# Weight pieces get tiles of their own, order and engines are written down step by step, and constant products fill TensorE's early gaps

## The chip, the cores and the metric

One core of one Trainium2 chip runs the kernel. The metric is the device time of one execution in microseconds; for the kernel before it is the median of three runs. A profile is taken of one execution.

## What is computed

Three parts follow each other, all in float32: attention with a mask of blocks of 64, a channel mix, and a token and channel mixer.

```python
def _attn_ref(q, k, v) -> np.ndarray:
    B, H, S, D = q.shape
    block = 64
    scale = 1.0 / np.sqrt(D)
    scores = scale * np.matmul(q, k.transpose(0, 1, 3, 2))
...
    mask = block_i >= block_j
    scores = np.where(mask, scores, -1000000000.0)
    scores = scores - np.max(scores, axis=-1, keepdims=True)
    attn = np.exp(scores)
    attn = attn / (np.sum(attn, axis=-1, keepdims=True) + 1e-09)
    return np.matmul(attn, v).astype(np.float32)
...
def _moe_ref(x, mu_k, mu_r, w_k, w_v, w_r) -> np.ndarray:
    B, S, D = x.shape
    x_prev = np.concatenate([np.zeros((B, 1, D), dtype=np.float32), x[:, :-1, :]], axis=1)
    xk = mu_k * x + (1.0 - mu_k) * x_prev
    xr = mu_r * x + (1.0 - mu_r) * x_prev
    k = np.maximum(xk @ w_k, 0.0)
    v = k * k @ w_v
    r = 1.0 / (1.0 + np.exp(-(xr @ w_r)))
    return (r * v).astype(np.float32)
...
def _moe2_ref(x, w_tok1, w_tok2, w_ch1, w_ch2) -> np.ndarray:
    xt = x.transpose(0, 2, 1)
    h = np.maximum(xt @ w_tok1, 0.0) @ w_tok2
    u = x + h.transpose(0, 2, 1)
    h2 = np.maximum(u @ w_ch1, 0.0) @ w_ch2
    return (u + h2).astype(np.float32)
```

The sizes are B = 4, H = 8, S = 576, D = 64; the model width is 512, the channel mix is 1024 wide, the mixer 256 over tokens and 1536 over channels.

## The kernel before

**Arithmetic.** A float32 product is made from parts: an operand is split into a high part that TensorE takes at its fast rate and a low part, the rest. Each group then takes three products: high by high (`mm_high`, L1024), low by high (`mm_low`, L1029) and high by low. `L1037` is the same for the others. VectorE, ScalarE and POOL make the parts: `xh` is a cast (L1005), `xl` a subtraction (L1009).

**Attention.** A batch is taken in two halves of the tokens, and each of them in four pairs of heads (`a000` to `a313`: batch, half, pair). A unit of a pair goes: scores on TensorE into `s` (L729), mask (L758), largest (L764), its negative as bias `nb` (L771, L773), exponentials on ScalarE into `p` (L783), sums (L791, L796), reciprocal (L802), the scaled high and rest in half precision into `pin` (L808, L814), a transposing DMA into `pt`, and the products with `vb` (L911). For the first half of batch 0 the probabilities are instead turned on TensorE by a diagonal `dg` of the reciprocal sums (L835 on POOL or L837 on VectorE, rotation L844, eviction `tf` L849, products L901). `vb` is v scaled by a power of two that is found from its largest value: a diagonal `vd` on POOL (L623), a gather on TensorE (L629), short scalings on VectorE. The sums go into `xt`, and `mix` makes `xk` and `xr` out of it (L993, L999, L1005, L1009).

**Mixing and mixer.** Channel mix (`channel_mix`), then for each batch the token part of the mixer (`front`), and for five stretches of tokens the channel part (`back`). These are most of TensorE's work.

**Weights.** `load_split` stages a matrix piece by piece: `split_chunk` loads a piece as three bytes a value (L552), casts its top part (L559), joins it with the rest on VectorE (L562), casts the high part (L568) and subtracts for the low part (L571). The first two matrices (`w_r`, `w_k`) have pieces of 410 columns and use memory that later holds `kh` and `kl`, four places in two tiles (`place`, `homes`); `w_v` uses `qkl`.

**What sets the order.** No engine's code is written in its final order. Each operation is a `step` with an engine, a cost and a key, and `Plan.schedule` gives each engine, step by step, what is ready and has the lowest key, with a model of costs, buffers, queues and TensorE's two speeds. `Plan.run` then writes the instructions in order of the planned starts. The keys come from due times that are worked out from tables in `PLAN` (`shift`, `fine`, `lead_begin` and others), and whether VectorE or another engine takes an operation from shares.

Of the kernel before, what the change touches and what calls it, by code (L numbers as in the profile page):

```python
# [39 lines left out]
SHARED = {"top", "join", "high", "low", "first", "second", "two", "diag", "here", "k_high", "k_low", "rest", "bias", "sums", "power"}  # L40

PLAN = dict(
    wr=-88.407, cpr=3.57, qt=2.2538, a0=87.407, lead=60.32, sh=0.57, xr=13.29, xk=-2.9382, cs=410, cv=256, wk=-50.94,
    wv=-0.88, cpk=1.6637, cpv=2.1596, p1_act=(0, 1, 2, 3, 4), p1_first=(0, 1, 2, 3, 4), xl_d=(0, 2), kl_d=(1, 3, 5),
    kh_a=(1, 2, 4, 6, 7), xh_d=(1, 3), mp=(), qk_a=(0, 1), ql_d=(0, 1), sh_r=(0.0733, 0, 0), sh_k=(0, 0, 0.58),
    sh_v=(0.02, 0, 0), sh_m=(0.35, 0, 0.41), first=38.34, sq_v=(), sq_a=(1, 2, 5, 6), p_ps=(1,), p_pf=(), nb_a=(1, 4),
    sm_a=(1,), ot_a=(1,), nq=(0, 1), dg_a=(), dg_g=(1,), ev_a=(0, 1), sq_1=(), fifo=("xh", "xl", "l", "o", "xt0",
    "xt1", "qkh", "uh"), ft=3.02, fd=27.39, cw=3.3876, tfr=23.04, lx=0.15, lpe=0.2, lse=0.12, land=2.31,

    fine={  # L50
        "a000": {"attention.edge": 28.99, "load_qk.whole": 3.33, "load_v_early.early": 1.77, "pv.products": -27.39,
        "pv.total": -40.77, "unit.bias": 16.3, "unit.diag": -28.96, "unit.evict": 42.0, "unit.exps": -9.13,
        "unit.inverse": -14.81, "unit.largest": 43.59, "unit.mask": 21.28, "unit.rotate": -0.91, "unit.scores": 16.31,
        "unit.sums": 46.99},
        "a001": {"attention.edge": -15.34, "load_qk.whole": 11.15, "load_v_early.early": 20.2, "pv.products": -0.07,
        "pv.total": 5.35, "unit.bias": 12.43, "unit.diag": 10.15, "unit.exps": -0.52, "unit.inverse": -12.18,
        "unit.largest": -6.57, "unit.mask": -0.59, "unit.rotate": 0.51, "unit.scores": 61.26, "unit.sums": -42.15},
        "a002": {"attention.edge": -2.39, "load_qk.whole": 1.24, "load_v_early.early": -81.65, "pv.products": -1.83,
        "pv.total": 2.38, "unit.bias": -19.03, "unit.diag": 6.6, "unit.evict": 7.45, "unit.exps": -1.93,
        "unit.inverse": 0.62, "unit.largest": -54.46, "unit.mask": 85.09, "unit.rotate": -12.99, "unit.scores": 23.8,  # L60
        "unit.sums": 87.92},
        "a003": {"attention.edge": -20.22, "load_qk.whole": -9.52, "load_v_early.early": -59.81, "pv.products": 36.55,
        "pv.total": 14.52, "unit.bias": 4.07, "unit.diag": 1.45, "unit.exps": -6.02, "unit.inverse": -86.56,
        "unit.largest": 2.37, "unit.mask": 7.52, "unit.rotate": -47.64, "unit.scores": -6.87, "unit.sums": 186.98},
        "a010": {"attention.edge": 5.12, "load_qk.whole": 9.68, "load_v.gather": 33.57, "load_v.largest": -4.86,
        "load_v.load": -4.39, "load_v.one": -28.07, "load_v.power": -78.48, "load_v.scale": -1.59, "load_v.spread":
        37.85, "load_v.two": 31.18, "pv.products": -2.0, "pv.total": 68.43, "unit.bias": -0.69, "unit.exps": -18.8,
        "unit.first": 176.41, "unit.inverse": 2.98, "unit.largest": 7.85, "unit.mask": 2.4, "unit.scores": 1.17,
        "unit.second": 0.37, "unit.sums": -4.36, "unit.turn": 49.55},
        "a011": {"attention.edge": 5.78, "load_qk.whole": -0.1, "load_v.gather": -0.4, "load_v.load": -13.43,  # L70
        "load_v.one": 0.85, "load_v.power": 31.47, "load_v.scale": -24.07, "load_v.spread": 10.15, "load_v.two":
        -40.58, "pv.products": 8.74, "pv.total": -0.55, "unit.bias": 16.5, "unit.exps": 22.85, "unit.first": 23.58,
        "unit.inverse": -15.47, "unit.largest": -9.04, "unit.mask": -10.34, "unit.scores": 0.48, "unit.second": -3.54,
        "unit.sums": 26.67, "unit.turn": 50.3},
        "a012": {"attention.edge": 3.0, "load_qk.whole": -23.78, "load_v.gather": -36.47, "load_v.largest": -0.16,
        "load_v.load": -9.38, "load_v.one": 9.22, "load_v.power": 13.36, "load_v.scale": 37.23, "load_v.spread":
        24.22, "pv.products": -4.89, "pv.total": -6.71, "unit.bias": 6.93, "unit.exps": 39.76, "unit.first": 9.47,
        "unit.inverse": 18.71, "unit.largest": -15.32, "unit.mask": 6.23, "unit.scores": -0.44, "unit.second": 123.91,
        "unit.sums": 51.69, "unit.turn": -18.01},
        "a013": {"attention.edge": 17.9, "load_qk.whole": 4.76, "load_v.gather": 1.97, "load_v.largest": 0.17,  # L80
# [1562 lines left out]
```

## Time and profile before

| | us |
|---|---|
| median of three runs | 804.49 (804.41 to 807.11) |
| the profiled execution: span from the first to the last instruction | 802.7 |
| what lies around the span (median less span) | 1.8 |
| TensorE busy in the span | 768.6 |
| VectorE busy | 470.9 |
| ScalarE busy | 416.0 |
| POOL busy | 155.1 |

The profile is of one execution, so terms that are read from it make up its span, and the 1.8 us is added to come to a run's time. TensorE is PE in the rows, VectorE DVE, ScalarE ACT. Busy times are the union of an engine's instructions, a wait is idle time with the instruction that ended it, and in a timeline like instructions that follow each other stand as one row. A tile's number is left out of its name.

### The profile page before, as it was taken

How to read it: one execution, taken by the hardware profiler on the slowest of the kernel's cores; microseconds unless marked ns; L12 is line 12 of the kernel's file. 1: busy time of each engine (PE TensorE's matmuls, PEld its weight loads, DVE VectorE, ACT ScalarE, POOL GpSimd, SP SyncE). 2: the span in 40 equal slices, each digit the busy share in tenths (PEclk: the TensorE clock that was granted, in tenths of full speed). 3: DMA queues.
4: the chain of work that ended last, by engine and by line, in shares of the span. 5: the costliest groups of instructions: out<-in, count | busy, mean ns of one | idle time of the engine just before them, and what ended most of it. 6: DMA issues, size and time to landing. Idle time of an engine off the chain costs nothing.

```text
span 802.7 us, 16092 instructions
## 1 busy us (share of the span) xinstructions
PE 768.6 (96%) x6120; PEld 665.8 (83%) x6120; DVE 470.9 (59%) x1189; ACT 416.0 (52%) x1074; POOL 155.1 (19%) x202
## 2 busy tenths in 40 slices
PE   5469999999999999999999999999999999999998
PEld 3246898889998999999989889998888888888886
DVE  7898898899998789882654588612211302301210
ACT  6887978788879787883555565502101201300100
POOL 5532322212124032322424122200000000000000
PEclk9987999999999999999999999999999999999999
DMA  8849946676858777453542745200000010000001
GB/s 287 293 132 162 190 116 141 122 169 121 170 126 124 142 138 172 75 88 80 202 147 88 267 125 150 75 27 1 14 27 1 17 36 14 1 26 14 1 26 40
DMA packets 130670, 83.25 MB, mean 104 GB/s; under 512 B 104352, under 2 KB 112160, under 8 KB 130080
## 3 DMA queue, kind: packets, MB, share of 16 engines
q1 hardware_dynamic: 130592, 82.22, 42.1%
q8 instruction: 48, 0.79, 0.4%
q14 instruction: 30, 0.25, 0.1%
HBM read 48.11 MB, written 9.44 MB: 72 GB/s over the span
## 4 chain that ended last, share of the span: by engine, by line
PE 85%; ACT 6%; DMA 4%; DVE 4%; issue 1%; POOL 0%; SPq 0%; DVEq 0%; ACTq 0%; POOLq 0%
PE b L1037 37%; PE l L1024 20%; PE l L1029 10%; PE s L729 5%; PE o L911 5%; PE b L1232 3%; PE b L1211 3%; ACT p L783 1%; DMA wst<-in_w_k 1%; DMA x<-xd 1%; PE b L1187 1%; DVE pin L814 1%; DVE nm L764 1%; DMA qkf<-in_kq 1%; DMA pt<-pin 1%
## 5 line engine op out<-in xcount | busy, mean ns | idle before, releaser
L1303 ACT ACTIVATE wy<-b 128x512 fp32r<-128x512 f32 (+1 forms) x60 | 33.3, 555 | 212.1 <-PE b L1037 210.8
L1037 PE MATMUL b<-uh,wx 128*128 128x512 f32 (+1 forms) x480 | 139.3, 372 | 0.0
L1024 PE MATMUL l<-xh,wx 128*128 128x256 f32 (+1 forms) x768 | 124.7, 302 | 0.8 <-DVE ve L635 0.4
L1024 PEld LDWEIGHTS l<-xh,wx 128*128 128x128 f32 x768 | 108.2, 189 | 6.8 <-issue 2.1
L1037 PE MATMUL b<-wy,c2a 128*128 128x512 f32 (+1 forms) x460 | 110.6, 367 | 0.0
L1037 PEld LDWEIGHTS b<-uh,wx 128*128 128x128 f32 x480 | 87.3, 188 | 17.3 <-issue 0.2
L1037 PEld LDWEIGHTS b<-wy,c2a 128*128 128x128 f32 x460 | 79.2, 189 | 15.3
L1318 DVE TENSOR_TENSOR x<-b,x 128x256 f32<-128x256 f32 (+7 forms) x32 | 13.5, 454 | 118.7 <-PE b L1037 118.7
L1024 PE MATMUL l<-kh,wy 128*128 128x256 f32 (+1 forms) x512 | 76.6, 299 | 0.1
L1037 PE MATMUL b<-gx,wx 128*128 128x512 f32 x192 | 75.4, 393 | 0.0
L783 ACT ACTIVATE p<-s,nb 128x128 f32<-128x128 f32 (+4 forms) x120 | 67.5, 566 | 11.6 <-DVE nb L773 6.0
L814 DVE SCALAR_TENSOR_TENSOR pin<-p,rs,pin 128x384 f16<-128x384 f32 (+3 forms) x104 | 66.6, 660 | 9.6 <-ACT pin L808 8.9
L1024 PEld LDWEIGHTS l<-kh,wy 128*128 128x128 f32 x512 | 69.9, 189 | 2.3 <-issue 0.9
L1029 PE MATMUL l<-xl,wx 128*128 128x320 f32 (+1 forms) x384 | 67.8, 298 | 0.0
L808 ACT ACTIVATE pin<-p,rs 128x384 f16<-128x384 f32 (+3 forms) x104 | 62.1, 622 | 9.1 <-DMA pt<-pin 5.8
L764 DVE TENSOR_REDUCE nm<-s 128x2 f32<-128x256 f32 (+4 forms) x80 | 63.8, 800 | 3.5 <-PE s L729 2.8
L1029 PEld LDWEIGHTS l<-xl,wx 128*128 128x128 f32 x384 | 56.1, 188 | 3.0 <-issue 2.4
L1306 DVE SCALAR_TENSOR_TENSOR wy<-b,wy 128x512 fp32r<-128x512 f32 (+1 forms) x28 | 16.1, 576 | 69.0 <-ACT wy L1303 68.9
L911 PEld LDWEIGHTS <-vb 128*64 128x64 f16 x1824 | 46.8, 113 | 9.9 <-issue 6.8
L911 PE MATMUL o<-pt,vb 128*64 128x128 f16 (+1 forms) x1824 | 53.3, 215 | 0.7 <-DMA pt<-pin 0.7
L1121 POOL TENSOR_TENSOR kl<-kt,kh 128x256 fp32r<-128x256 f32 (+1 forms) x40 | 35.1, 881 | 65.7 <-ACT kh L1118 40.5
L1009 POOL TENSOR_TENSOR xl<-mt,xh 128x256 fp32r<-128x256 f32 (+1 forms) x32 | 30.2, 944 | 87.5 <-DVE xh L1005 40.7
(123 smaller groups left out, 1385.5 us busy)
## 6 DMA issues: line engine op xcount, KB each, us to landing
wst<-in_w_c SPq DMA_DIRECT2D x24, 256.0 KB, 2.8
qkf<-in_kq SPq DMA_DIRECT2D x12, 480.0 KB, 4.4
v<-in_v SPq DMA_DIRECT2D x16, 320.0 KB, 3.1
x<-xd SPq DMA_DIRECT2D x4, 1152.0 KB, 8.1
wst<-in_w_c2a SPq DMA_DIRECT2D x18, 256.0 KB, 3.1
qkl<-in_w_v SPq DMA_DIRECT2D x16, 256.0 KB, 3.8
wst<-in_w_k SPq DMA_DIRECT2D x9, 410.0 KB, 4.1
qkf<-in_kq SPq DMA_DIRECT2D x12, 256.0 KB, 2.9
```

The source lines that it names most:

```text
L729: self.nc.tensor.matmul(o, q[e, q0:q0 + P], k[e, k0:k1], start=n == 0, stop=n == len(terms) - 1)
L764: nc.vector.tensor_reduce(out=c["nm"][:, :nh], in_=m, axis=AX.XY if j == 4 else AX.X, op=ALU.max, negate=True)
L783: nc.scalar.activation(out=c[x], in_=s, func=AF.Exp, scale=0.125, bias=c["nb"][:, x:x + 1], accum_out=c["sm"][:, x:x + 1],)
L808: nc.scalar.activation(out=like(pin[:, :n]), in_=c[x], func=AF.Copy, scale=rs)
L814: nc.vector.scalar_tensor_tensor(out=like(pin[:, w:w + n]), in0=c[x], scalar=rs, in1=like(pin[:, :n]), op0=ALU.mult, op1=ALU.subtract)
L911: nc.tensor.matmul(o[hh * D:hh * D + D, q0:q0 + rows], v[:, i, y, hh, :], st["pt", hh, j][:, x * (j + 1) + i, :], start=i == x == y == 0, ...
L1009: (nc.vector if i in pl["xl_d"] else nc.gpsimd).tensor_tensor(out=l, in0=x[i], in1=raw(x["h"][i]), op=ALU.subtract)
L1024: self.nc.tensor.matmul(ps, ww[:, k, :], x[0][k], start=k == 0 and n == 0, stop=False)
L1029: self.nc.tensor.matmul(ps, w[0][:, k, :], x[1][k], start=False, stop=k == kt - 1)
L1037: self.nc.tensor.matmul(ps, ww[k], xx[k], start=k == 0 and n == 0, stop=k == kt - 1 and n == 2)
L1121: (nc.vector if m in pl["kl_d"] else nc.gpsimd).tensor_tensor(out=part("kl")[:, m, :], in0=c["q", m], in1=raw(c["kh"][:, m, :]), op=ALU.su ...
L1303: nc.scalar.activation(out=gh(m), in_=d["g", m][:, :n], func=AF.Relu)
```

## The change

Its parts, in the order of the diff below:

- The tables of `PLAN` and the keys go. Each step has a number, and two lists have an entry for each number: `RANK` is its key, and `ON` the engine letter of the steps that may run on more than one (`"any"`). The helpers `copy`, `less` and `scale` write the operation for the engine that is named.
- The model of TensorE's two speeds goes out of `schedule`.
- `Plan.run` takes a function `fill`. Where TensorE's plan has a gap before a step, until 90 us of the plan, it calls `fill` once for each 0.085 us of the gap beyond 0.15. A fill is a product of ones (128 x 128) by ones (128 x 192, bf16) into columns 320 to 511 of an accumulator `o` that no step reads or writes.
- The pieces of `w_r` and `w_k` get three tiles of their own (`stage0` to `stage2`) in place of four places in the memory of `kh` and `kl`.
- The accumulators `o` are two named tiles; the DMA scratch is 1024.

```diff
+FILL = (4.0, 90.0)
...
+RANK = [int(x) for x in """
+15 0 23 3 5 12 17 21 6 7 1 9 2 35 24 28 29 33 36 37 39 44 46 50 49 54 59 26 31 34 40 57 42 61 75 79 82 80 85 94
...
+ON = "".join("""
+-----------------V--A-A-A-A---V--A-A-A-A---A-----A--A-A-A-A---A--A-A-A-V---A-----A--V-V-A-A---A--A-A-V-A---A----
...
-    def step(self, eng, cost, key, fn, *args, r=(), w=(), after=(), hold=(), dma=0.0, alone=False, mode=""):
+    def step(self, eng, cost, fn, *args, r=(), w=(), after=(), hold=(), dma=0.0, alone=False, mode=""):
...
-            key -= PLAN["lead_begin"].get(kind, 0.0)
-        key -= PLAN["fine"].get(self.group, {}).get(kind, 0.0)
-        s = Step(len(self.steps), eng, cost, key - PLAN["shift"].get(self.group, 0.0), fn, args, dma)
-        s.kind, s.group = kind, self.group
-        s.shared, s.mode = shared, mode
+        alts = None
+        if eng == "any":
+            alts = cost
+            eng = ON[n] if ON else next(iter(alts))
+            cost = alts[eng]
+        share = lambda e: e == "G" or e == "V" and name[-1] in SHARED and not alone
+        s = Step(n, eng, cost, RANK[n] if RANK else n, fn, args, dma)
+        s.kind, s.group = f"{name[1]}.{name[-1]}" if len(name) > 2 else "", self.group
+        s.alts, s.shares = alts, share
+        s.shared, s.mode = share(eng), mode
...
-    def run(self):
-        order = self.schedule()
-        for s in order:
-            s.fn(*s.args)
+    def run(self, fill):
+        last, until = FILL
+        for s in self.schedule():
+            if s.eng == "PE":
+                for _ in range(int((min(s.start, until) - last - 0.15) / 0.085)):
+                    fill()
+                last = s.end
+            s.fn(*s.args, *(s.eng if s.alts else ()))
 
...
+    def copy(self, e, out, x):
+        (self.nc.scalar.copy if e == "A" else self.nc.vector.tensor_copy)(out, x)
+
+    def less(self, e, out, a, b):
+        (self.nc.vector if e == "V" else self.nc.gpsimd).tensor_tensor(out=out, in0=a, in1=b, op=ALU.subtract)
+
...
-        def low():
-            (nc.vector if low_v else nc.gpsimd).tensor_tensor(
-                out=part(1), in0=s["mid"].bitcast(F32), in1=raw(part(0)), op=ALU.subtract
-            )
+        def low(e):
+            self.less(e, part(1), s["mid"].bitcast(F32), raw(part(0)))
...
-        step(*(("V", c_v(k)) if low_v else ("G", c_g(k))), key, low, r=[z] + t[0], w=t[1])
+        step("any", both(v=c_v(k), g=c_g(k)), low, r=[z] + t[0], w=t[1])
 
...
-        self.ones = pool.tile([P, P], BF16, name="ones", bufs=1)
+        self.ones = pool.tile([P, 512 - NT], BF16, name="ones", bufs=1)
+        self.o = [self.ps_o.tile([P, 512], F32, name=f"o{x}", bufs=1) for x in range(BUFS["o"])]
...
+    def fill(self):
+        self.nc.tensor.matmul(self.o[0][:, NT:], self.ones[:, :P], self.ones, start=True, stop=True)
...
-        homes = [Buf(tag) for tag in ("kh", "kl")]
-        tiles = {}
-        half = NF * NT // 2
-        turns = itertools.cycle(range(4))
-
-        def place(x):
-            a = x // 2
-            if a not in tiles:
-                tiles[a] = self.mp.tile([P, NF * NT], U32, tag=("kh", "kl")[a], name="wst", bufs=1)
-            return tiles[a][:, x % 2 * half:(x % 2 + 1) * half]
-
-        def spare(x):
-            return place(x)[:, half - pl["cs"]:]
-
-        for x in range(4):
-            step("G", 0.3, -1e3, lambda x=x: nc.gpsimd.memset(spare(x), 0), w=[(homes[x // 2], ("t", x % 2))])
+        cs = CS
+        turns = itertools.cycle(range(NSTAGE))
+        self.stage = [self.ap.tile([P, 3 * cs + 2], U32, name=f"stage{x}") for x in range(NSTAGE)]
+        for x, z in enumerate(self.stage):
+            step("G", 0.3, nc.gpsimd.memset, z[:, 2 * cs + 2:], 0, w=[(f"stage{x}", "t")])
 
         def early():
             x = next(turns)
-            return lambda: place(x), (homes[x // 2], x % 2), lambda: spare(x), (homes[x // 2], ("t", x % 2))
+            z = self.stage[x]
+            return lambda: z, (f"stage{x}", "z"), lambda: z[:, 2 * cs + 2:], (f"stage{x}", "t")
 
         def staged(pool, tag, size):
...
-        self.plan.run()
+        self.plan.run(self.fill)
...
+NSTAGE = 3
...
-    nc = bacc.Bacc("TRN2", target_bir_lowering=False, num_devices=1)
+    nc = bacc.Bacc("TRN2", target_bir_lowering=False, num_devices=1, dynamic_dma_scratch_size=1024)
```

The instructions move as follows; each place is shown before and after.

The first is TensorE's queue where the first mixing product stands (`L1024` before, `L928` after; both `mm_high`); these are six rows of before from the last products of the first half's attention on. `pt` is a transposed probability tile.

```order
L911 MATMUL o<-pt_637,vb 64x128
L729 MATMUL s<-qk 128x512 x2
L729 MATMUL s<-qk 128x288 x2
L1024 MATMUL l<-xh,wx 128x256 x4
L911 LDWEIGHTS vb
L911 MATMUL o<-pt_678,vb 64x128
```

After, the same place has fills (`L538`, their operands `ones` and their tile `o_90`), and the products with `pt` stand behind the mixing product.

```order
L538 MATMUL o_90<-ones 128x192
L670 MATMUL s<-qk 128x512 x2
L538 LDWEIGHTS ones
L538 MATMUL o_90<-ones 128x192
L928 MATMUL l<-xh,wx 128x256 x16
L835 LDWEIGHTS vb
L835 MATMUL o_90<-pt_733,vb 64x128
```

In all, 195 fills stand on TensorE's queue, 187 of them ahead of this first mixing product; two scores of 288 columns, a set of 24 products with `vb` and one gather have moved from before it to behind it.

The second place is ScalarE's beginning, before: the table load, the first exponentials of `p`, then the first cast of a staged piece `wst`.

```order
L783 ACT_TABLE_LOAD
L783 ACTIVATE p,sm<-s,nb 128x128 x2
L559 CAST wst<-wst 128x410
L771 ACTIVATE nb<-nm 128x2
L783 ACTIVATE p,sm<-s,nb 128x256
```

After, the same beginning.

```order
L467 ACT_TABLE_LOAD
L467 CAST stage_96<-stage_96 128x410
L723 ACTIVATE p,sm<-s,nb 128x128 x2
L731 ACTIVATE rs<-sm 128x2
L723 ACTIVATE p,sm<-s,nb 128x256
L474 ACTIVATE dg<-eye,rs 128x128 x2
L467 CAST stage_98<-stage_98 128x410
```

The cast of the first piece has moved ahead of the exponentials, the table load stands with it, and two diagonals `dg` have come onto ScalarE.

The third is POOL behind its first memory fills, before: diagonals in turn with the low parts `wx` of the staged pieces.

```order
L623 TENSOR_SCALAR vd<-eye,vm 128x128
L835 TENSOR_SCALAR dg<-eye,rs 128x128
L571 TENSOR_TENSOR wx<-wst,wx 128x410 x2
L835 TENSOR_SCALAR dg<-eye,rs 128x128
L571 TENSOR_TENSOR wx<-wst,wx 128x410 x2
L571 TENSOR_TENSOR wy<-qkl,wy 128x256
```

After, the same place.

```order
L566 TENSOR_SCALAR vd<-eye,vm 128x128
L478 TENSOR_SCALAR dg<-eye,rs 128x128 x2
L470 TENSOR_TENSOR wy<-qkl,wy 128x256
L566 TENSOR_SCALAR vd<-eye,vm 128x128
L470 TENSOR_TENSOR wx<-stage_98,wx 128x410
```

Low parts of `w_r` and `w_k` have left POOL for VectorE all but one, and the second `vd` comes earlier in POOL's queue. POOL's whole list goes from 202 instructions to 143. VectorE's 145th instruction was the last input of the first mixing product before; after, its 121st and a cast on ScalarE are. Joins ahead of it fall from 24 to 19, instructions that scale and round `v` from 27 to 14, and low parts rise from five to twelve.

## Rows read from the trace of the kernel before

**Rows 1.** Page, head and part 1: busy time, share, instructions.
```profile
span 802.7 us, 16092 instructions
...
PE 768.6 (96%) x6120; PEld 665.8 (83%) x6120; DVE 470.9 (59%) x1189; ACT 416.0 (52%) x1074; POOL 155.1 (19%) x202
```

**Rows 2.** Stretches to 64.4 and from 70: busy time of each engine, granted clock.
```profile
0.00:64.40 64.40, 36.88 (x179) 22.52 (x180) 54.73 (x148) 48.99 (x134) 29.47 (x44) 0.92 0.72 231
70.00:803.00 733.00, 726.11 (x5891) 638.30 (x5889) 412.32 (x1029) 363.41 (x931) 125.30 (x158) 1.00 0.40 92
```

**Rows 3.** Waits of TensorE: total us, times, longest.
```profile
PE l L629 <- POOL vd L623: 9.8, 2, 9.0
PE s L729 <- ACT p L783: 8.9, 11, 2.3
PE s L729 <- DMA qk<-in_kq: 4.3, 1, 4.3
```

**Rows 4.** Timeline of TensorE, 40 to 80: start, us, operation.
```profile
40.24 0.26 PE L629 MATMUL l<-vd,ones 128*128 128x128 bf16 x1 [9.00 <-POOL vd L623]
40.34 2.05 PE L844 MATMUL l<-dg,p 128*128 128x128 f32 x8
...
48.29 1.13 PE L844 MATMUL l<-dg,p 128*128 128x128 f32 x8 [0.71 <-DVE dg L837]
...
59.63 2.08 PE L729 MATMUL s<-qk 64*128 64x512 f32 x4 [0.66 <-ACT p L783]
...
64.47 1.47 PE L1024 MATMUL l<-xh,wx 128*128 128x256 f32 x4
65.87 1.92 PE L911 MATMUL o<-pt,vb 128*64 128x128 f16 x32
...
71.69 1.13 PE L729 MATMUL s<-qk 64*128 64x512 f32 x4
...
74.36 0.86 PE L911 MATMUL o<-pt,vb 128*64 128x128 f16 x24
...
75.73 1.13 PE L729 MATMUL s<-qk 128*128 128x288 f32 x4
```

**Rows 5.** Stretches inside the front, and 70 to 360, columns as in Rows 2.
```profile
4.30:43.00 38.70, 22.68 (x100) 15.21 (x102) 31.25 (x83) 31.52 (x88) 20.43 (x24) 1.00 0.83 286
56.00:64.40 8.40, 5.93 (x34) 3.13 (x33) 8.11 (x20) 5.78 (x15) 1.62 (x2) 0.50 0.65 139
0.00:63.00 63.00, 35.48 (x176) 21.55 (x177) 53.37 (x145) 48.99 (x134) 28.74 (x43) 0.93 0.73 234
70.00:360.00 290.00, 288.35 (x3369) 260.82 (x3368) 257.37 (x704) 241.24 (x654) 77.96 (x96) 1.00 0.70 137
```

**Rows 6.** Chain that ended last, 441 to 445: start, us, piece.
```profile
441.94 2.35 PE l L1024 x16
```

**Rows 7.** Groups by shape: busy us, mean ns, idle before and its releaser.
```profile
L796 DVE TENSOR_SCALAR rs<-sm 128x2 f32<-128x2 f32 x48 | 12.1, 252 | 7.8 <-ACT p L783 7.5
L814 DVE SCALAR_TENSOR_TENSOR pin<-p,rs,pin 128x576 f16<-128x576 f32 x16 | 13.0, 810 | 5.4 <-ACT pin L808 5.2
...
L571 POOL TENSOR_TENSOR wx<-wst,wx 128x410 fp32r<-128x410 f32 x8 | 9.3, 1176 | 4.2 <-ACT wx L568 4.2
```

**Rows 8.** Timelines of POOL and VectorE at 20, VectorE at 47.
```profile
19.75 2.14 POOL L571 TENSOR_TENSOR wx<-wst,wx 128x408 fp32r<-128x408 f32 x2 [0.49 <-ACT wx L568]
...
20.80 1.37 DVE L999 SCALAR_TENSOR_TENSOR mt<-xt,mu,mt 128x256 f32<-128x256 f32 x1
...
47.02 0.48 DVE L999 SCALAR_TENSOR_TENSOR mt<-xt,mu,mt 128x256 f32<-128x256 f32 x1
```

**Rows 9.** Waits of VectorE to 63, columns as in Rows 3.
```profile
DVE wst L562 <- ACT wst L559: 3.1, 5, 1.7
```

**Rows 10.** Timeline of ScalarE, its first 10 us.
```profile
6.13 1.28 ACT L783 ACT_TABLE_LOAD   x1 [6.13 <-DVE nb L773]
...
8.94 0.65 ACT L559 CAST wst<-wst 128x410 f16<-128x410 bf16 x1 [0.71 <-DMA wst<-in_w_r]
```

More of the change, by code (lines that the diff above doesn't have):

```diff
@@ L305 @@
+SHARED = {"top", "join", "high", "low", "first", "second", "two", "diag", "here", "k_high", "k_low", "rest", "bias", "sums", "power",
+          "shifted", "square", "one"}
+FILL = (4.0, 90.0)
+FIFO = ("xh", "xl", "l", "o", "xt0", "xt1", "qkh", "uh")
+CS, CV = 410, 256
+LX, LPE, LSE, LAND = 0.15, 0.2, 0.12, 2.31
 BUFS = dict(
@@ L333, in c_g, with both @@
     return 0.15 + 0.0021 * n
+def both(a=None, v=None, g=None):
+    return {k: x for k, x in (("A", a), ("V", v), ("G", g)) if x is not None}
 class Buf:
@@ L411, in schedule @@
         parked = {}
-        queue = {tag: [] for tag in PLAN["fifo"]}
+        queue = {tag: [] for tag in FIFO}
         for s in self.steps:
@@ L420, in schedule @@
             q.sort(key=lambda b: b.key, reverse=True)
-        ring = window = busy = port = 0.0
-        warm, mode = False, None
+        ring = port = 0.0
+        mode = None
         push = lambda s: heapq.heappush(pend[s.eng], (s.ready, s.n, s))
@@ L518, in __init__, with load_split @@
         self.cover = {}
-    def load_split(self, key, dt, name, dst, n, block, stage, size, src, share, gate=()):
+    def load_split(self, name, dst, n, block, stage, size, src, gate=()):
         self.plan.group = name
@@ L628, in gather @@
             c["a"] = self.ps_l.tile([P, 512], F32, tag="l", name="l")
-            nc.tensor.matmul(c["a"][:, :P], self.ones, c["d"], start=True, stop=True)
+            nc.tensor.matmul(c["a"][:, :P], self.ones[:, :P], c["d"], start=True, stop=True)
         def scale(k):
@@ L689, in load_qk @@
         c = {}
-        if b == 0 and hf in PLAN["nq"]:
+        if b == 0:
             h = Buf("qkh")
@@ L1013, in mix @@
-            k = key + dt * i
-            step(*(("G", c_g(n)) if i in pl["mp"] else ("A", c_a(n, ap=True))), k, shifted, r=[txts[i], "omu"], w=[tm], hold=[th, tl])
-            step("V", c_v(n, True), k, here, r=[txts[i], tm], w=[tm])
-            step(*(("V", c_v2(n)) if i in pl["xh_d"] else ("A", c_a(n))), k, high, r=[tm], w=[th])
-            step(*(("V", c_v(n)) if i in pl["xl_d"] else ("G", c_g(n))), k, low, r=[tm, th], w=[tl])
+                self.less(e, l, x[i], raw(x["h"][i]))
+            step("any", both(c_a(n, ap=True), c_v2(n) + 0.06), shifted, r=[txts[i], "omu"], w=[tm], hold=[th, tl])
@@ L1018, in mix @@
+            step("V", c_v(n, True), here, r=[txts[i], tm], w=[tm])
+            step("any", both(c_a(n), c_v2(n)), high, r=[tm], w=[th])
+            step("any", both(v=c_v(n), g=c_g(n)), low, r=[tm, th], w=[tl])
         return x
@@ L1244, in front @@
         add = lambda *a, **k: steps.append(step(*a, **k))
-        add("S", 0.475, key - 6.0, load, r=gate + [f"xd{b}"], w=[tx], dma=3.28)
+        add("S", 0.475, load, r=gate + [f"xd{b}"], w=[tx], dma=3.28)
         tps = [Buf("b") for _ in range(2)]
```

728 lines of the change are left out of this document (209 added, 519 removed), and 154 rows, old and new, of tables (RANK, shift).

## The prediction, made before the changed kernel ran

> **What bounds the kernel now.** The page's first part comes first: TensorE is busy 768.6 of 802.7 us, every other engine under 60% [rows 1]. So the span is TensorE's work plus the time in which it has none. The stretches say where that is: in the first 64.4 us TensorE works 36.88, VectorE 54.73 and ScalarE 48.99; in the 733 us from 70 on TensorE stands still for 6.9 [rows 2]. TensorE's waits name what was late in the front: the diagonal `vd` of POOL (9.8, one wait of 9.0), ScalarE's exponentials (8.9), the first `qk` (4.3, until then nothing can start) [rows 3].
>
> A second loss hides in the busy time. The same four scores of 512 columns take 2.08 us at 59.6 and 1.13 at 71.7, eight rotations 2.05 at 40.3 and 1.13 at 48.3: the short ones are 0.55 of the long ones [rows 4]. For 56 to 64.4 the granted clock says 0.50, the lower level (1.2 GHz); for 4.3 to 43 it says 1.00, but the rotations at 40.34, behind a wait of 9 us, have the long duration [rows 4, 5]. I trust durations and count both stretches as the lower level: 22.68 + 5.93 = 28.6 us of TensorE, of which 0.45 x 28.6 = 12.9 is lost [rows 5]; the first mixing product and the set of products behind it (1.47 + 1.92 [rows 4]) lose another 1.5 by the same ratio. Work at 2.4 GHz is 768.6 - 12.9 - 1.5 = **754.2**.
>
> The sum for before: its first mixing product starts at 64.47 [rows 4]. TensorE has by then done 36.88 - 12.9 = 24.0 of useful work [rows 2], so it is 40.5 behind. 40.5 + 754.2 + 1.5 + 6.6 (what it stands still from 70 to the end, 732.7 - 726.1) = 802.8, against a span of 802.7. The run's time was 1.8 above its span (804.5, the median), which I add at the end.
>
> From 64.47 on TensorE never stops for long, because mixing work is there for whatever attention is late with. So the change is worth what it moves that start, less what it loses behind it.
>
> **The fill products.** The order has 195 of them, 187 ahead of the first mixing product, 8 behind. None is in the trace. The nearest row is a series of sixteen products of 320 columns in 2.35 us, 147 ns each [rows 6]; by columns 192 take 88 ns, at the lower level 176. I take 88 (at most 8 x 0.088 = 0.7 us lands where TensorE is the bound). Below that a fill cannot save anything; above it stands the lone gather of 128 columns with 0.26 [rows 4], start and all. What hides them are the 64.47 - 36.88 = 27.6 us in which TensorE stands still in the front. TensorE's queue alone would reach the first mixing product at 4.3 + 20.6 (useful work, below) + 187 x 0.088 = 16.5 + 2 (some 4 us at the lower level before the rise, as from 40.24 [rows 4], 0.45 of it lost) = **43.4**.
> That they raise the clock I take from 40 to 48: TensorE works from 40.24 with hardly a gap, and the rotations fall from 2.05 to 1.13 [rows 4]. The Trainium skill, "TensorE: Matmul & The Clock Gate" (What's actually happening), states that the array starts throttled and activity releases it. The durations agree, the granted clock of 1.00 in 4.3 to 43 doesn't; were that column right, TensorE's queue would end at 53.6 and the sum would be 799 instead of the one below.
>
> **What stands ahead of the first mixing product.** Two 288-column scores, a set of 24 products and one gather move behind it: 2 x 1.13 + 0.86 + 0.26 = 3.4 [rows 4], so useful work ahead of it is 24.0 - 3.4 = 20.6. Before, its last input was a cast of `xh` that VectorE starts just before 63, its 145th instruction; of these 63 us VectorE was busy 53.37 [rows 5]. In the order of after the same product needs VectorE's 121st and then a cast on ScalarE. I priced both lists by the mean of each instruction's form in the groups by shape: before 55.6 (trace: 53.4), after 47.8. The larger pieces: joins fall from 24 to 19; `v` work falls from 27 instructions to 14; low parts rise from five to twelve. Scaled by the trace, 47.8 x 53.4 / 55.6 = 45.9.
> POOL has 28.74 us of work in this stretch [rows 5], after some 12 by the same pricing, as low parts of 410 columns, 1176 ns each there, change engine [rows 7]. While one such low part ran on POOL, from 19.75, VectorE's 256-column mix took 1.37 us; with nothing on POOL, at 47.02, 0.48 [rows 8]. Two such delays of 0.9 go: 45.9 - 2 = 44. By the Trainium skill, "SBUF — State Buffer" (Who interferes with whom), VectorE with two operands in SBUF and a reading GpSimd exclude each other for a whole instruction; the rows agree, and with all of VectorE's excess over the means gone the sum would be 792.
> VectorE's idle time there was 63 - 53.4 = 9.6, of which 3.1 stood behind the casts of staged weights [rows 9]. Staging now has three tiles of its own instead of four in the memory of `kh` and `kl`, and scores come at twice the rate; nothing shows how much idle the new order leaves, so it lies between 0 and 9.6. I take 4.1, a little under the middle, and 0.4 for the cast: the first mixing product starts at **48.5** (43.4, TensorE's floor, to 45.9 + 9.6 = 55.5).
>
> **ScalarE's first instruction** is now a cast that waits for the first w_r piece, and the exponentials stand behind it. Before, the table load began at 6.13, and the cast of the first piece waited for its transfer until 8.94 [rows 10]. So the first exponentials may be up to 2 us late; that is part of the 4.1.
>
> **Behind the first mixing product.** VectorE's share rises: its steps up to the last pin come to 361 us by form means instead of 343, 18 more, for POOL's smaller one. From 70 to 360 VectorE was busy 257.37 of 290, 32.6 idle, and TensorE waited 1.65 in it [rows 5]. As attention starts 16 us earlier, its slack is about used up: I charge 3 us of new waits of TensorE (0 to 8). The staging memory costs no instruction. The 6.6 of other idle time stays.
>
> **Sum:** (48.5 - 20.6) = 27.9 behind, + 754.2 + 6.6 + 0.7 + 3 = 792.4; + 1.8 = **794.2 us**.
>
> **Rivals.**
> - *The plan's gaps hold.* VectorE's waits vanish, the start is TensorE's floor, no late charge: 22.8 + 754.2 + 6.6 + 0.7 + 1.8 = **786**. For it: the fills are counted from the planned gaps and end there. Against: VectorE alone has 44 us of work to do by then. Chance 0.17.
> - *The front's chain stays as it is.* VectorE keeps its 9.6 idle, the start is 55.5, and VectorE's later load costs 5: 34.9 + 754.2 + 6.6 + 0.7 + 5 + 1.8 = **803**, no change. For it: 8.9 of TensorE's waits ended at ScalarE's exponentials [rows 3], and most of these still stand ahead of the first mixing product. Chance 0.12.
> - *VectorE becomes the bound (slower).* Its 32.6 us of idle from 70 to 360 pay for the 18 us shifted onto it and for the 16 by which mixing starts earlier, which leaves nothing; if half of the old idle is unavoidable (behind ScalarE alone it stood 7.5 us at the sums and 5.2 at the pins of 576 columns, over the whole span [rows 7]), the attention ends 16 us later than TensorE needs it: 794 + 16 = **810**. It decides above 10.4 us of lateness. Against: TensorE has other batches' products to put in between, and waited only 1.65 in that stretch. Chance 0.08.
> - *The fills don't raise the clock.* Then each takes 0.176 and useful work stays at 20.6 / 0.55 = 37.5: the queue reaches the first mixing product at 4.3 + 37.5 + 32.9 = 74.7, and the sum is 74.7 + (754.2 - 20.6) + 6.6 + 1.4 + 3 + 1.8 = **821**, slower. Against: the rise at 43 followed products with smaller gaps than these. Chance 0.03.
>
> **How the numbers follow.** The forecast has the remaining 0.60 and, with the start between 45 and 55 and the later charge between 0 and 6, its own range is 787 to 803. A measurement of this kernel can tell about 0.5%, 4 us: faster is below 800.5, slower above 808.5. Faster: 0.17 and 0.57 of the forecast's 0.60, 0.74, and what of the third case lies lower, 0.01: 0.75. Same: the third case's 0.11 and 0.03 of the forecast: 0.14. Slower: 0.08 + 0.03 = 0.11. The range reaches from the second case's lower side (784, VectorE a little under its price) to the third with its late charge (805); some 0.2 lie outside.
>
> **What would show it.** Right: rotations and scores of the front at their short durations from about 8 us on, fills near 88 ns, the first mixing product between 45 and 53, VectorE over 85% busy until then, TensorE's still time behind 70 under 12 us. Wrong: long durations behind the fills; a first mixing product past 55 with VectorE waiting for ScalarE or a staging transfer; TensorE waiting for pins or exponentials between 70 and 390, or VectorE at 95% there.

## Result and the profile after

The changed kernel took 792.41 us (median of four runs, 791.18 to 794.63), the kernel before beside it 805.8 (804.41 to 809.38): an estimated ratio of 0.9845, with a 95% interval of 0.9809 to 0.9881 (dividing the two medians gives 0.9834; the ratios below are such estimates too). In a second set it took 792.86 against 805.92, ratio 0.9839 (0.9817 to 0.9862). The forecast was 794.

The head and part 1 of the page of the changed kernel; they answer to [rows 1].

```profile
span 791.8 us, 16348 instructions
...
PE 770.0 (97%) x6315; PEld 673.3 (85%) x6315; DVE 499.9 (63%) x1311; ACT 374.3 (47%) x1010; POOL 116.7 (15%) x143
```

TensorE is 97% busy in a shorter span, but 195 fills are in its 770.0. VectorE has 29 us more than before, ScalarE 42 and POOL 38 less.

Stretches of the changed kernel; the first ends where its first mixing product starts, and the columns are those of [rows 2].

```profile
0.00:45.09 45.09, 37.78 (x333) 27.97 (x334) 41.53 (x124) 38.83 (x125) 10.88 (x22) 1.00 0.79 258
45.09:72.00 26.91, 25.76 (x329) 21.09 (x329) 25.87 (x80) 25.02 (x72) 5.28 (x8) 1.00 1.05 215
72.00:200.00 128.00, 120.62 (x1456) 109.74 (x1452) 116.79 (x325) 101.26 (x291) 32.24 (x36) 0.99 0.74 144
200.00:300.00 100.00, 97.86 (x1131) 89.21 (x1131) 93.68 (x267) 72.47 (x209) 20.62 (x22) 1.00 0.73 143
...
420.00:791.80 371.80, 367.99 (x1866) 311.61 (x1865) 129.35 (x296) 72.72 (x156) 18.31 (x23) 1.00 0.16 50
```

The first row is the gain: the start of mixing moved by 19.4 us, from 64.47 to 45.09. Two engines' lists got shorter up to there. VectorE had 54.73 us of work before [rows 2] and has 41.53 now; it stood still 9.7 and now 3.6. ScalarE had 48.99 [rows 2] and has 38.83; it stood still 15.5 and now 6.3. Each is a full account of the same 19.4 us, so neither sum says by itself which engine set the start. Both are nearly full now: ScalarE works 38.83 of the 39.92 us from its first instruction at 5.17 on (97%), VectorE 92% of the whole stretch.

In the kernel before, the chain that ended last runs through both as well. From 13.4 us to the scores at 62.80 it lies 26.4 us on ScalarE, 11.3 on VectorE and 9.9 in two transfers of staged `w_k` pieces, and its last link ahead of the scores is an exponential:

```profile
62.17 0.58 ACT p L783 x2
...
62.80 2.29 PE s L729 x4
```

The rows from 72 to 300 are what was given back: TensorE stands still 7.4 + 2.1 us there, where it stood still 1.65 in the whole of 70 to 360 before [rows 5]. VectorE is 92% busy in them (88% in the same stretch before).

TensorE's timeline in the front of the changed kernel, to set beside [rows 4].

```profile
4.08 1.65 PE L670 MATMUL s<-qk 64*128 64x128 f32 x8 [4.08 <-DMA qk<-in_kq]
5.67 2.81 PE L538 MATMUL o<-ones 128*128 128x192 bf16 x21
8.41 0.70 PE L670 MATMUL s<-qk 64*128 64x256 f32 x4
...
13.24 1.16 PE L774 MATMUL l<-dg,p 128*128 128x128 f32 x8 [0.24 <-ACT dg L474]
...
39.72 3.80 PE L538 MATMUL o<-ones 128*128 128x192 bf16 x44
43.91 1.13 PE L670 MATMUL s<-qk 64*128 64x512 f32 x4 [0.38 <-ACT p L723]
...
45.09 2.16 PE L928 MATMUL l<-xh,wx 128*128 128x256 f32 x16
```

From 8.41 on scores, rotations and mixing products have their short durations: scores of 256 columns 0.70 (1.22 before at 11.7), eight rotations 1.16, the first mixing products 16 in 2.16 where the first four took 1.47 in [rows 4]. No pause is longer than 0.6 us. A fill in a series takes 3.80 / 44 = 86 ns. The row at 43.91 says that the fills did not set the start: they were through, and the last scores ahead of mixing waited 0.38 for an exponential of ScalarE. The last input of the first mixing product came at the same time, a cast that ScalarE started 0.2 after VectorE had its part ready:

```profile
44.01 0.47 DVE L906 SCALAR_TENSOR_TENSOR mt<-xt,mu,mt 128x256 f32<-128x256 f32 x1
```

```profile
44.68 0.42 ACT L467 CAST xh<-mt 128x256 fp32r<-128x256 f32 x1
```

TensorE's waits, total, times, longest; they answer to [rows 3].

```profile
PE o L835 <- DMA pt<-pin: 5.2, 6, 1.4
PE s L670 <- ACT p L723: 4.2, 8, 1.8
...
PE l L928 <- DVE r L1035: 1.7, 2, 1.5
```

The 9.8 us for `vd` are gone and the exponentials cost 4.2 in place of 8.9; new are 5.2 us for transposed tiles `pt` (0.7 before), all of it between 72 and 200.

ScalarE's first rows, as in [rows 10].

```profile
5.17 1.28 ACT L467 ACT_TABLE_LOAD   x1 [5.17 <-DMA stage<-in_w_r]
6.46 0.65 ACT L467 CAST stage<-stage 128x410 f16<-128x410 bf16 x1
6.99 0.35 ACT L723 ACTIVATE p<-s,nb 128x128 f32<-128x128 f32 x1
```

The first exponential comes at 6.99, earlier than before (7.43): the piece that the cast waits for has landed at 5.17, as its load stands third in the transfer queue now.

### The profile page after: what moved, and what is told of

Its sections match the earlier page's. It is cut to its first block, busy times and chain, and to the rows that moved or that the text cites. A ratio compares the mean times of both kernels' runs of the same rounds, so it can differ in the third digit from the quotient of the medians.

```text
span 791.8 us, 16348 instructions
## 1 busy us (share of the span) xinstructions
PE 770.0 (97%) x6315; PEld 673.3 (85%) x6315; DVE 499.9 (63%) x1311; ACT 374.3 (47%) x1010; POOL 116.7 (15%) x143
## 4 chain that ended last, share of the span: by engine, by line
PE 67%; DVE 9%; DMA 4%; ACT 2%; issue 1%; ACTq 0%; DVEq 0%; SPq 0%
PE b L941 38%; PE l L928 11%; PE l L933 6%; PE b L1090 4%; PE b L1111 3%; DMA pt<-pin 3%; DVE pin L750 2%; PE s L670 2%; PE o L835 2%; DVE nm L704 1%; PE b L1066 1%; DVE mt L906 1%; ACT p L723 1%; DVE xl L470 0%; DVE r L1035 0%
## 5 line engine op out<-in xcount | busy, mean ns | idle before, releaser
L941 PE MATMUL b<-uh,wx 128*128 128x512 f32 (+1 forms) x480 | 142.5, 373 | 0.0
L928 PE MATMUL l<-xh,wx 128*128 128x256 f32 (+1 forms) x768 | 124.4, 302 | 1.8 <-DVE r L1035 1.5
L928 PEld LDWEIGHTS l<-xh,wx 128*128 128x128 f32 x768 | 108.4, 190 | 8.5 <-DVE r L1035 1.7
L928 PE MATMUL l<-kh,wy 128*128 128x256 f32 (+1 forms) x512 | 76.6, 299 | 0.3 <-DVE r L1035 0.2
L928 PEld LDWEIGHTS l<-kh,wy 128*128 128x128 f32 x512 | 70.3, 189 | 3.2 <-issue 1.2
L723 ACT ACTIVATE p<-s,nb 128x384 f32<-128x384 f32 (+4 forms) x120 | 67.4, 564 | 11.3 <-DVE nb L476 5.2
L1181 DVE SCALAR_TENSOR_TENSOR gx<-b,wy 128x512 fp32r<-128x512 f32 x32 | 21.8, 690 | 67.7 <-ACT wy L1178 67.7
L474 ACT ACTIVATE pin<-p,rs 128x512 f16<-128x512 f32 (+3 forms) x78 | 48.9, 638 | 15.2 <-DVE rs L742 6.8
L835 PEld LDWEIGHTS <-vb 128*64 128x64 f16 x1824 | 45.2, 111 | 12.6 <-issue 10.1
L835 PE MATMUL o<-pt,vb 128*64 128x128 f16 (+1 forms) x1824 | 50.6, 212 | 5.3 <-DMA pt<-pin 5.2
L941 PEld LDWEIGHTS b<-gx,wx 128*128 128x128 f32 x192 | 36.1, 188 | 8.3
```

What stands on the lines that cost most here:

```text
L474: self.nc.scalar.activation(out=out, in_=x, func=AF.Copy, scale=by)
L723: nc.scalar.activation(out=c[x], in_=s, func=AF.Exp, scale=0.125, bias=c["nb"][:, x:x + 1], accum_out=c["sm"][:, x:x + 1],)
L835: nc.tensor.matmul(o[hh * D:hh * D + D, q0:q0 + rows], v[:, i, y, hh, :], st["pt", hh, j][:, x * (j + 1) + i, :], start=i == x == y == 0, ...
L928: self.nc.tensor.matmul(ps, ww[:, k, :], x[0][k], start=k == 0 and n == 0, stop=False)
L941: self.nc.tensor.matmul(ps, ww[k], xx[k], start=k == 0 and n == 0, stop=k == kt - 1 and n == 2)
L1181: nc.vector.scalar_tensor_tensor(out=gl(m), in0=d["g", m][:, :n], scalar=0.0, in1=raw(gh(m)), op0=ALU.max, op1=ALU.subtract)
```

## The experiments

**Without fills.** Order, engines and staging are those of the changed kernel.

```diff
-FILL = (4.0, 90.0)
+FILL = (4.0, 0.0)
```

> The changed kernel without its 195 fills; order, engines and staging are the same instruction by instruction. Theory (order and engines): VectorE and ScalarE set when the first mixing product can start, the fills only let TensorE keep pace. TensorE then works at the lower level in the front, its 21.7 us of useful work take up to 39, and each set of scores and rotations is up to 1 us longer; the first mixing product comes at 46 to 51 in place of 45.1 and the time is 793 to 798. Rival (the clock is the gain): the start goes back to 55 or later and the time to 801 or more.

798.39 us (795.43 to 800.83), 0.9945 of before (0.9924 to 0.9965). Timeline of TensorE in its front:

```profile
31.08 2.08 PE L774 MATMUL l<-dg,p 128*128 128x128 f32 x8 [2.22 <-ACT dg L474]
...
40.72 1.13 PE L670 MATMUL s<-qk 64*128 64x512 f32 x4
...
46.90 2.08 PE L670 MATMUL s<-qk 64*128 64x512 f32 x4 [4.17 <-ACT p L723]
48.91 3.68 PE L928 MATMUL l<-xh,wx 128*128 128x256 f32 x16
```

The lower level is back in most of the front (2.08 for the rotations at 31.08, 3.68 for sixteen mixing products), though not in all of it (1.13 for the scores at 40.72), the waits are longer, and mixing starts at 48.91. The theory had 46 to 51 and 793 to 798; the start fits, the time is 0.4 past that range. VectorE's work ahead of the start is the same 41.5 (next row), so its share of the 3.8 us is idle time, which fits a slower TensorE that hands on its results later.

```profile
0.00:48.91 48.91, 29.62 (x146) 18.31 (x146) 41.55 (x124) 40.51 (x126) 11.21 (x23) 0.90 0.74 239
```

By the ratios to before (0.9945 here, 0.9845 and 0.9839 with fills) the fills are worth 1.0 to 1.1% of the time on this order, and order, engines and staging without them 0.55% (0.7% by dividing medians). The profiled execution is the fastest of the four, so its span of 793.7 shows less of the difference than the medians do.

**Fills alone, in the order before.**

```diff
-        order = self.schedule()
-        for s in order:
+        last, until = FILL
+        for s in self.schedule():
+            if s.eng == "PE":
+                for _ in range(int((min(s.start, until) - last - 0.15) / 0.085)):
+                    fill()
+                last = s.end
             s.fn(*s.args)
...
```

The accumulators `o` become two named tiles here as in the change, so that the fills have columns to write.

> The kernel before with fills put into the gaps of its own plan up to 90 us (244 of them), its order, engines and staging unchanged. Theory (order and engines): TensorE's busy time in the front becomes short again, but the first mixing product waits for the same VectorE instruction, at 60 or later in place of 64.5; the time is 799 to 803. Rival (the clock is the gain): the start comes to 52 or earlier and the time to 794 or less.

806.18 us (804.95 to 809.63), 1.0019 of before (0.9985 to 1.0053): no change. Rotations in the front, TensorE's first mixing product, and the stretch to it:

```profile
42.74 1.11 PE L855 MATMUL l<-dg,p 128*128 128x128 f32 x8
...
66.57 1.47 PE L1035 MATMUL l<-xh,wx 128*128 128x256 f32 x4
```

```profile
0.00:66.57 66.57, 51.50 (x424) 39.14 (x424) 54.10 (x148) 49.23 (x135) 30.18 (x44) 0.93 0.71 224
```

TensorE is 51.50 us busy to there in place of 36.88, the rotations behind the long wait are short (2.05 before [rows 4]), and mixing starts no earlier: VectorE has the same 54 us to do and ScalarE the same 49. The first mixing products are at the lower level again (1.47, as before), behind a wait of 1.75 for an exponential. The start (60 or later) went with the theory, the 799 to 803 did not; short durations in most of the front were worth nothing here. Of the two parts the fills alone are worth nothing, the rest alone 0.55%, and together they give 1.6%.

**One wait of before taken away.** The load of the second `v` 9 us earlier, its largest value, power and `vd` 8 us earlier, in the old order.

```diff
-        for s in order:
+        back = {"load_v.load": 9.0, "load_v.largest": 8.0, "load_v.power": 8.0, "load_v.spread": 8.0}
+        at = lambda s: s.start - (back.get(s.kind, 0.0) if s.group == "a011" else 0.0)
+        for s in sorted(order, key=lambda s: (at(s), s.eng == "X", s.n)):
...
```

> The kernel before with one chain taken earlier: the load of the second v goes 9 us earlier in the transfer queue, and its largest value, power of two and diagonal vd 8 us earlier on VectorE and POOL (a second tile for v, room for it from the DMA scratch); all else stands in the old order. It takes away the wait of 9.0 us of TensorE for vd. Theory (VectorE's and ScalarE's staging work sets the start of mixing, and TensorE's wait only lay beside it): the wait shrinks to 2 us or less, but the first mixing product comes at 61 or later and the time is 800 to 806. Rival (the wait itself held the front up): the start comes at 58 or earlier and the time is 798 or less.

807.36 us (802.91 to 809.23), 1.0023 (1.0005 to 1.0042). The rows on which it rests:

```profile
33.15 0.27 PE L631 MATMUL l<-vd,ones 128*128 128x128 bf16 x1 [2.14 <-POOL vd L625]
33.25 2.05 PE L846 MATMUL l<-dg,p 128*128 128x128 f32 x8
42.68 1.65 PE L731 MATMUL s<-qk 64*128 64x384 f32 x4 [7.38 <-ACT p L785]
...
67.63 1.47 PE L1026 MATMUL l<-xh,wx 128*128 128x256 f32 x4
```

ScalarE in the same run:

```profile
32.00 0.36 ACT L785 ACTIVATE p<-s,nb 128x128 f32<-128x128 f32 x1
...
33.38 0.46 ACT L561 CAST tw<-qkl 128x256 f16<-128x256 bf16 x1
...
41.85 0.42 ACT L570 CAST wy<-qkl 128x256 fp32r<-128x256 f32 x1
42.17 0.36 ACT L785 ACTIVATE p<-s,nb 128x128 f32<-128x128 f32 x1
```

The wait of 9.0 for `vd` is 2.1, and 7.4 us stand at the next scores instead: they start at 42.68, and at 42.45 in the kernel before. They wait for an exponential, and from 33.38 to 42.17 ScalarE has none in its queue: it runs fifteen casts of staged weights there. Mixing starts at 67.63, 3.2 later than before. The longest wait of [rows 3] was a wait beside other work, as the theory had it; the time is 1.4 past its range.

**Ten low parts back on POOL,** at the same places of the new order.

```diff
-            s.fn(*s.args, *(s.eng if s.alts else ()))
+            s.fn(*s.args, *(MOVES.get(s.n, s.eng) if s.alts else ()))
...
+MOVES = dict.fromkeys((144, 149, 154, 159, 164, 169, 174, 179, 189, 194), "G")
```

> The changed kernel with ten low parts of the first two weight matrices on POOL in place of VectorE, at the same places of the written order. Theory (VectorE's queue bounds the front and the whole of it was a gain to take the work off POOL because the two engines hinder each other): VectorE's work falls by ten times 0.59 us, but its two-operand instructions beside POOL's get longer by as much; the start stays within 2 us of 45.1 or later, the time is 791 to 796. Rival (VectorE is simply overloaded): the start comes 3 us earlier or the later waits shrink, 789 or less.

796.75 us (795.2 to 800.4), 0.9921 (0.9893 to 0.9948): some 0.8% slower than the changed kernel by the ratios, whose intervals do not touch, and 0.75 us past the theory's range. The start is at 46.30 (45.09 and 46.02 in the two profiles of the changed kernel). VectorE's groups by shape to 60 us, first of the changed kernel, then of this one:

```profile
L470 DVE TENSOR_TENSOR wx<-stage,wx 128x410 fp32r<-128x410 f32 x12 | 7.1, 589 | 0.0
...
L506 DVE SCALAR_TENSOR_TENSOR qkl<-qkl,tw 128x256 uint32<-128x256 uint32 x9 | 3.7, 414 | 0.2 <-issue 0.2
...
L596 DVE SCALAR_TENSOR_TENSOR vb<-v,vs,vb 128x640 f16<-128x640 f32 x2 | 1.8, 882 | 0.0
```

```profile
L507 DVE SCALAR_TENSOR_TENSOR qkl<-qkl,tw 128x256 uint32<-128x256 uint32 x9 | 5.4, 599 | 0.0
...
L597 DVE SCALAR_TENSOR_TENSOR vb<-v,vs,vb 128x640 f16<-128x640 f32 x2 | 2.6, 1321 | 0.0
L471 DVE TENSOR_TENSOR wx<-stage,wx 128x410 fp32r<-128x410 f32 x3 | 2.5, 845 | 0.0
```

Ten low parts less at 589 ns should save 5.9 us, but the joins beside them go from 414 to 599 ns, `vb` from 882 to 1321 and the three low parts left from 589 to 845. Not every form suffers: the joins of 410 columns go from 580 to 610, and the mix (L906) falls from 544 to 484. VectorE's busy time to 60 us falls by 1.7 only (55.64 to 53.92). The Trainium skill, "SBUF — State Buffer" (Who interferes with whom), states that a VectorE instruction with two operands in SBUF and a reading GpSimd instruction shut each other out. These rows agree.

**The same move in the order before.**

```diff
-            (nc.vector if low_v else nc.gpsimd).tensor_tensor(
+            (nc.vector if low_v or tok[0] in ("wr", "wk") else nc.gpsimd).tensor_tensor(
```

> The kernel before with all low parts of the first two weight matrices on VectorE, ten of them taken off POOL, at the same places of the old order; nothing else. Theory (the choice of engines is part of the gain only with an order made for it): VectorE gains 6 us of work and loses the delays beside POOL, the first mixing product stays within 3 us of 64.5, 802 to 808. Rival (POOL's low parts held the front up): the start comes at 59 or earlier and the time falls to 799 or less.

804.71 us (802.69 to 806.83), 1.0007 (0.9991 to 1.0024). Its first mixing product:

```profile
64.38 0.85 PE L1024 MATMUL l<-xh,wx 128*128 128x256 f32 x4
```

```profile
0.00:64.38 64.38, 36.32 (x179) 21.99 (x180) 54.28 (x157) 48.97 (x134) 18.32 (x34) 0.79 0.74 229
```

64.38 against 64.47: the engine of the low parts moves nothing in an order that was written for the other one. VectorE ran nine instructions more to there, yet its work is 54.28 in place of 54.73 [rows 2]: its other instructions got shorter by as much, the joins of 410 columns from 618 to 573 ns and the mix from 646 to 534. So this run did not make VectorE's list longer, and it can't tell whether that list sets the start.

**Staging memory, both ways.** In the changed kernel the three places go back into the memory of `kh` and `kl`.

```diff
-        self.stage = [self.ap.tile([P, 3 * cs + 2], U32, name=f"stage{x}") for x in range(NSTAGE)]
+                tiles[a] = self.mp.tile([P, NF * NT], U32, tag=("kh", "kl")[a], name="wst", bufs=1)
...
```

> The changed kernel with the three staging places back in the memory of kh and kl (the planner gives the same order up to the third group of mixing products, 194 fills). Theory (memory of its own lets the first mixing products run while the second matrix is still staged, to 57 us): the start stays at 45, but the first high part of kh, planned at 52, must wait for the last staged piece, TensorE waits some 5 us more between 50 and 75 and the time is 795 to 799. Rival (where the pieces lie is worth nothing): 791 to 794.

793.57 us (791.83 to 794.48), 0.9848 (0.9826 to 0.9869), beside 0.9839 of the changed kernel on the same chip: the theory fell. The start is where it was:

```profile
45.26 2.14 PE L928 MATMUL l<-xh,wx 128*128 128x256 f32 x16
```

The other way round, three tiles of their own in the kernel before (the diff above read backwards, with the DMA scratch of the change):

> The kernel before with three staging tiles of their own in place of the memory of kh and kl; its keys are unchanged, but its planner now puts three sets of attention products ahead of the first mixing product. Theory (the place of the staging memory is worth little without the new order): 801 to 808. Rival (the staging memory held the front up): the long wait of TensorE for vd shrinks by 4 us or more and the time falls to 798 or less.

831.84 us (829.88 to 834.46), 1.0353 (1.0326 to 1.0379), far outside both expectations. Its planner orders three sets of attention products ahead of mixing; the rows:

```profile
74.64 1.21 PE L1027 MATMUL l<-xh,wx 128*128 128x256 f32 x8
```

```profile
PE s L732 <- ACT p L786: 16.8, 13, 4.8
```

Mixing starts at 74.64, and TensorE waits 16.8 us for exponentials. As the order moved with the memory, this run can't price the memory; it shows that the planner's order together with the memory can cost 3.5%. The run above it shows that in the new order the place is worth nothing that can be measured.

**Half the fills.**

```diff
-                for _ in range(int((min(s.start, until) - last - 0.15) / 0.085)):
+                for _ in range(int((min(s.start, until) - last - 0.15) / 0.17)):
```

> The changed kernel with one fill for each 0.17 us of a planned gap, 92 in all in place of 195. Theory (TensorE's pauses in the front need only be broken up, not filled): the durations in the front stay at the higher level, the start within 1.5 us of 45.1, 791 to 795. Rival (each fill taken away is time at the lower level): the start between those of 195 and of no fills or later, 47 to 49, and 795 to 798.

794.97 us (792.76 to 796.98), 0.9867 (0.9845 to 0.9888), beside the changed kernel in the same set:

> The changed kernel once more, beside the three below on one chip. 790 to 795, 0.981 to 0.988 of before.

792.86 us (790.97 to 794.58), as expected. The intervals of the two overlap, so the 2 us are not certain. The stretches of the half:

```profile
20.00:40.00 20.00, 16.09 (x113) 10.17 (x115) 19.13 (x55) 19.42 (x66) 5.44 (x8) 0.91 0.78 263
```

The granted clock is 0.91 from 20 to 40 (1.00 with all fills), TensorE waits 7.1 for exponentials in place of 3.1, and mixing still starts at 45.74 (46.02 in the other's profile): most of the worth is there with 92 fills. Start and time are those of the theory; its durations are not quite, as the granted clock says.

**What is given back: three attempts on it.** Thirty first pins between 70 and 310 from VectorE to ScalarE, and fifteen low parts of q and k from VectorE to POOL, each at its old place.

```diff
+MOVES = dict.fromkeys((732, 720, 596,
...
...
+MOVES = dict.fromkeys((513, 697, 605,
...
```

> The changed kernel with 30 of VectorE's first pins between 70 and 310 us on ScalarE, at the same places of the written order. Theory (VectorE, 91 to 94% busy from 72 to 300, is what makes the pins late and TensorE wait for their transfers): VectorE loses some 10 us of work there, ScalarE gains 18 and is at 85%; TensorE's still time from 72 to 300 falls from 9.5 to 6 or less and the time to 787 to 791. Rival (the waits come from the transfers and from ScalarE's exponentials): no better, 793 to 799.

795.63 us (794.44 to 797.38), 0.9872 (0.9851 to 0.9893).

```profile
72.00:200.00 128.00, 119.14 (x1461) 107.04 (x1456) 113.98 (x309) 105.52 (x301) 31.45 (x36) 1.00 0.73 143
200.00:300.00 100.00, 97.13 (x1125) 88.33 (x1125) 89.04 (x250) 77.29 (x222) 19.42 (x23) 1.00 0.69 140
```

VectorE lost 7.4 us of work against the changed kernel (116.79 + 93.68), and TensorE stands still 11.7 in place of 9.5.

> The changed kernel with 15 low parts of the later q and k, between 70 and 310 us, on POOL in place of VectorE, at the same places of the written order. Theory (VectorE's load behind the first mixing product is what is given back): VectorE loses 10 us of work in 72 to 300, TensorE's 9.5 us of still time there falls by 3 or more, 788 to 790. Rival (POOL takes twice as long for each, stands in VectorE's way, and the scores wait for them): 793 to 798.

805.02 us (802.58 to 809.12), 1.0011 (0.9991 to 1.0030): the whole gain is gone. VectorE's busy time falls by 2.7 us, TensorE's by 6.4:

```profile
72.00:200.00 128.00, 116.66 (x1404) 104.36 (x1400) 116.99 (x303) 94.17 (x274) 42.26 (x42) 0.97 0.71 142
200.00:300.00 100.00, 95.42 (x1065) 86.72 (x1062) 90.77 (x249) 68.93 (x196) 29.77 (x26) 0.98 0.66 132
```

15.9 us of still time, and a time past both ranges. A low part of q and k takes 2.0 us on POOL (median) against 0.69 on VectorE, three times as long, and TensorE's long waits in this stretch are again for `pt` (6.0) and exponentials (2.9); the path between the two was not traced.

The third leaves the engines and tells the planner that `pt` lands later.

```diff
-                end = ring + LAND
+                end = ring + LAND + 1.3 * (s.kind == "unit.turn")
```

> The changed kernel with the planner told that a transposed tile pt lands 1.3 us later than it was told; its order is the same up to the first mixing product, behind it the products that read pt are written later and mixing work earlier (232 fills). Theory (the order places these products at the planned landing with no slack, so every late pin becomes a wait of TensorE): TensorE's 4 to 6 us of waits for pt shrink to 2 or less and the time is 787 to 791. Rival (attention is as late as it is, by VectorE's and ScalarE's work, and later products only push the wait on): 792 to 798.

813.64 us (812.2 to 815.73), 1.0114 (1.0089 to 1.0140). TensorE's waits:

```profile
PE s L670 <- ACT p L723: 6.2, 8, 3.8
...
PE l L928 <- DVE r L1035: 3.0, 3, 1.5
PE l L572 <- POOL vd L566: 2.8, 3, 1.3
PE o L835 <- DVE xt L476: 2.5, 1, 2.5
```

The waits for `pt` are no longer among the long ones, as the theory wanted, and others for exponentials, `r`, `vd` and `xt` came in their place. The last product that reads `pt` starts at 379.2 (359.2 in the changed kernel, 386.1 before), and the time is worse than both ranges. Its order differs behind the first mixing product throughout, so the run tells that this slack is no cure, not which wait costs what. All three theories fell.

## Why the forecast was right, and where it was not

The forecast of 794 and the measured 792.4 agree. The span shows that two terms were off against each other: 45.09 to the start, 732.2 of TensorE's work behind it and 14.5 of still time make 791.8, where the forecast had 48.5 + 734.3 + 9.6 = 792.4. The start came 3.4 earlier and the work behind it was 2.1 less, which hid 4.9 more of still time.

- **Fills, 88 ns each.** They took 86 in the series of 44; at that price 195 are 16.8 us. They hide: the start did not wait for them.
- **Useful work ahead of mixing, 20.6.** 37.78 - 187 x 0.086 = 21.7, an estimate; the first 21 fills took 2.81 us, 134 ns each, and with that it is 20.7.
- **The start, 48.5.** It was 45.09. VectorE's work to it came to 41.53 in place of 44 and its idle time to 3.6 in place of 4.5. That a shorter front moves the start held: with the fills alone both engines' work stays and so does the start, and with the longest wait of TensorE gone it stays too. That VectorE's list is the one that sets it is argued and not shown. The sum priced no list of ScalarE's, and ScalarE's got shorter by as much (10.2 of work, 9.2 of idle time) and was 97% full. The last input of the first mixing product waited for ScalarE too; and in the kernel before the cast that was named as the last input was done at 63.1, while the start at 64.47 stood behind scores that had waited for an exponential. No run shortened one list by much and left the other. The nearest is the one with ten low parts on POOL: VectorE has 0.9 less to do up to the start (40.63) and ScalarE the same (39.07), and the start is no earlier (46.30). That the sum came out near with VectorE alone is in part luck: both lists had shrunk alike.
- **Fewer delays beside POOL, 2 us.** That they are part of the shorter list is shown from both sides: ten low parts given back to POOL come back as longer instructions, and ten taken off POOL in the old order cost VectorE nothing.
- **What is lost behind the start, 3 on top of 6.6.** This term was mis-sized: it is 14.5 in all, 1.2 of it to 72, 9.5 from 72 to 300 and 3.8 behind 420. That is 7.9 in place of 3, at the very end of the 0 to 8 that was given for it. Behind 70 it is 13.4, past the 12 that was named as a sign of being right, and the waits for `pt` and exponentials between 70 and 390 (5.2 and 2.1) were named as a sign of being wrong.
- **Its reason, VectorE's 18 us more.** VectorE is indeed 92% busy from 72 to 300. But taking 7.4 us of work off it onto ScalarE did not help, POOL made it worse, and later planned landings only exchanged one wait for others. The fills are not the reason: without them TensorE stands still 8.1 us there. What makes these 9.5 us (8.3 in the second profile) is open: no run here isolates one cause, and an order with slack for VectorE and ScalarE together was not tried. Nor do the runs part the new order from the new engines in the 0.55%: of the engines only the low parts were tried alone, worth 0.8% with the fills in place, and the place of the staging memory was found to be worth nothing.
- **ScalarE's first cast, up to 2 us late.** It was not; the first piece landed 3.8 us sooner, and the exponentials came 0.4 earlier.
- **The clock.** The fills raised it, and on this order they are worth 1.0 to 1.1%. The forecast had no term of its own for that: it was inside VectorE's idle time of 4.1, with scores at twice the rate among its reasons. Without the fills that idle time is 48.91 - 41.55 = 7.4 in place of 3.6, which is the 3.8 us by which the start is later. Where the rest of the 1% lies no trace shows: the two profiled spans differ by 1.9 only.
- **The rivals.** The front's chain staying as it was (803), VectorE becoming the bound (810) and fills that don't raise the clock (821) did not happen; the planned gaps (786) held at the start, within 1.7 us of the floor of 43.4, but not behind it. What was set against the last rival, a rise behind products with smaller gaps than these, would speak for it; what decided is the short durations from 8.41 on.

## What to carry over

A long wait of the bounding engine is not worth its length: here 6.9 of 9.0 us were removed and 7.4 came back at the next instruction, because the engine that feeds it was no earlier. Read the busy time of every feeding engine up to the point that matters, not of one alone, and price a change by what it takes from there: two lists that shrink together give the same sum, and only a run that shortens one of them tells which sets the point. Filling gaps to hold the clock was worth nothing in one order and 1% in another, where the engines that feed TensorE were done earlier.
